# An attention block in two halves: a unit's products with V are issued three steps later, ahead of the next unit's turned maxima

## Chip, cores and metric

One core of one Trainium2 chip runs the whole kernel in one launch. The metric is the device time of an execution in microseconds (us). The kernel works in fp32, most products as three matmuls on upper and lower halves in fp32r.

## The reference, cut to what matters

```python
h = x + A(layernorm(x))            # S = 2048 tokens, D = 1024, H = 32 heads of 32, 4 segments of 512
# A, for each segment s and head:
logits = qs @ ks.T * scale + mask           # 512 x 512, causal
a_dot = softmax(logits) @ vs
a_mem = (phi(qs) @ M) / (phi(qs) @ z + 1e-6)   # M and z come from the segments before; 0 in segment 0
o = g * a_mem + (1 - g) * a_dot
M, z = M + phi(ks).T @ vs, z + phi(ks).sum()
# then o @ wo, and a block of layernorm, w1, gelu, w2 (channel MLP) over all tokens
```

## The kernel before

The sequence is done in two halves of 1,024 tokens. In each half the attention comes first, then the product with `wo`, then the MLP. The attention of a half has 16 **units** (n = 0 to 15), each one group of four heads (`g`) and one segment of 512 tokens (`sl` is 0 or 1). Units alternate so that segment 0 of a group comes before its segment 1. Segment `s = 2*half + sl`; only units with `s > 0` read the memory M. In the first half these are the eight units n = 2, 3, 5, 7, 9, 11, 14, 15; in the second half all sixteen.

The kernel's code is one long hand-written order. Every engine executes its instructions in program order. A unit has 24 **steps** (`b = 24 * n` is its first). In each step TensorE (PE) runs the three matmuls (`mm3`) of one of the 24 pieces of this unit's K, Q and V projections, and then `close(step)` runs what has been put down for that step with `at(step, ...)`, in the order in which it was put down: what unit n put down stands ahead of what unit n+1 put down. Last in `close` comes at most one small matmul from the list `small` (`one_small`). So the attention of a unit runs beside the projections of the units after it:

- `qk1` (steps 22 to 44 of the unit): logits of one block of rows into a PSUM bank "qk"; VectorE (DVE) adds the mask and takes the row maximum (L571); one step later ScalarE (ACT) takes exp for the row sums (L573).
- `lse` and `halves` (47, 48): logarithm of the sums, and the maxima in two halves `mh` (L601).
- `turn` (50): four matmuls turn `mh` into the tile `ptn` (L607), in one of two banks "pt". `rows` (51 to 54) copies it four times into rows 96 to 103 of `qs`, one copy a step, in turn by ACT, DVE, ACT, DVE (L610). Each copy waits for the one before it.
- `qk2` (53 to 67): logits again, transposed, with the maxima in the contraction (L619), into a bank "pst" of the same tag "pt"; ACT takes exp into `e` (L622); GpSimd (POOL) clears what the mask hides (L626). The first piece is in step 53, the second in step 54.
- `av` (71): sixteen products of `e` with V, 32 stationary columns each, one bank `po` (L633; four passes, so 32 matmul records of half a product each). `out` two steps on (73): DVE scales `po` by the gate and adds the memory's part (L642; L644 in segment 0). `out_high` (74): ACT copies the upper half (L651). `out_low` (75): POOL takes the lower half (L654). `store` (77): two DMAs by the queue of SP (L658), for n < 13.
- `reads` (26): puts four small matmuls `pm` on the list; after the second and the fourth, three DVE operations finish a half of the memory's part (L469 to L473).
- `stack` (steps 9 to 24): DMAs that lay K and Q of a head under each other (L417). `wload` (2, 7, 15 of every second unit): DMAs of weights (L688).

Step 71 of unit n is the step in which unit n+2 does its last piece of V's projection (step 23 of n+2). Step 74 is step 2 of unit n+3 and step 50 of unit n+1; unit n+2 is then at its step 26.

Of the kernel before, what the change touches and what calls it, by code (L numbers as in the profile page):

```python
# [39 lines left out]
LSE, TURN, ROWS, AV, LAST = 47, 50, (51, 52, 53, 54), 71, 432 + 8  # L40
# [11 lines left out]
def build(tc, x, wq, wk, wv, wo, beta, w1, b1, w2, b2, out):  # L52
# [307 lines left out]
    def attention(half, first):  # L360
# [15 lines left out]
        def at(step, *fns):  # L376
            assert step >= now[0], (step, now[0])
            todo.setdefault(step, []).extend(fns)
# [281 lines left out]
        def heads(u, b):  # L660
            for m, (j, i) in QK1.items():
                at(b + m, partial(qk1, u, j, i))
            at(b + QK0, partial(qk0, u))
            at(b + LSE, partial(lse, u))
            at(b + LSE + 1, partial(halves, u))
            at(b + TURN, partial(turn, u))
            for j, m in enumerate(ROWS):
                at(b + m, partial(rows, u, j))
            for m, (j, n) in QK2.items():
                at(b + m, partial(qk2, u, j, n))  # L670
            at(b + AV, partial(av, u))
            at(b + AV + 2, partial(out, u))
            at(b + AV + 3, partial(out_high, u))
            at(b + AV + 4, partial(out_low, u))
            if u["n"] < 13:
                at(b + AV + 6, partial(store, u))

        def close(step):

# [39 lines left out]
        for n in range(16):  # L719
            u = unit(n)  # L720
            heads(u, 24 * n)
            g, sl = ORDER[n]
            b = 24 * n
# [850 lines left out]
```

## Time and profile before

| | us |
|---|---|
| median of 3 runs (lowest, highest) | 2185.76 (2185.12, 2187.62) |
| the profiled execution | 2187.23 |
| its span, first to last instruction | 2185.5 |
| PE busy in the span | 2157.7 |

In the timelines a row is one instruction or several alike: its start in us from the span's start, how long it took, engine, line, operation, what it writes and reads, and in brackets how long the engine had been idle before and what ended that. A matmul of 512 columns has a row of 0.39 to 0.40 us, but the next one may start 0.23 us after it: rows of PE overlap, and only the distance between starts tells what a matmul takes. PEld is the loading of a matmul's stationary columns.

### The profile page before, as it was taken

The numbers are of one execution on the slowest core, as the hardware profiler recorded it, in microseconds if no ns is written. First come the engines' busy times: TensorE is split into PE (matmuls) and PEld (weight loads), VectorE is DVE, ScalarE is ACT, GpSimd is POOL, SyncE is SP. The second block draws the span as 40 slices with busy tenths as digits, with TensorE's granted clock in tenths as the row PEclk, the third lists the DMA queues.
The fourth block names the chain that finished last, engine by engine and source line by source line (L and its number), as shares of the span: only waits on it lengthen the run. The fifth ranks groups of instructions, "written<-read, shape, count | busy, mean of one in ns | idle before, by whom it ended". The sixth has DMA issues, their size and how long they took to land.

```text
span 2185.5 us, 33210 instructions
## 1 busy us (share of the span) xinstructions
PE 2157.7 (99%) x10937; PEld 1750.4 (80%) x10937; DVE 1349.0 (62%) x2696; ACT 1102.1 (50%) x2433; POOL 959.7 (44%) x1206
## 2 busy tenths in 40 slices
PE   7999999999999999999999999999999999999999
PEld 6777777778888888877777768888887888888887
DVE  6766666665745556766667655745666665576653
ACT  5777777762543445777777752643443232322221
POOL 5534345562444434533335561534446544256330
PEclk9999999999999999999999999999999999999999
DMA  6544445664465655544444663575569865676762
GB/s 182 134 106 107 105 107 136 190 203 164 154 207 155 187 158 147 136 107 109 106 108 133 198 197 141 173 217 162 171 199 373 274 226 185 190 244 230 250 222 92
DMA packets 352405, 376.20 MB, mean 172 GB/s; under 512 B 27214, under 2 KB 244330, under 8 KB 352234
## 3 DMA queue, kind: packets, MB, share of 16 engines
q1 hardware_dynamic: 288778, 336.98, 50.7%
q10 hardware_dynamic: 63456, 37.10, 5.6%
q8 instruction: 87, 1.43, 0.3%
q14 instruction: 84, 0.69, 0.1%
HBM read 241.27 MB, written 82.38 MB: 148 GB/s over the span
## 4 chain that ended last, share of the span: by engine, by line
PE 91%; DVE 2%; DMA 2%; POOL 2%; ACT 1%; issue 1%; SPq 0%; ACTq 0%; DVEq 0%; POOLq 0%
PE po L1410 22%; PE bps L1014 10%; PE cps L1014 7%; PE dps L1014 7%; PE pst L619 4%; PE po L633 3%; PE pqk L569 3%; PE kps L127 3%; PE vps L127 3%; PE qps L127 3%; PE kps L128 3%; PE pwo L127 2%; PE kps L129 2%; PE vps L128 2%; PE pwo L129 2%; PE pwo L128 2%
## 5 line engine op out<-in xcount | busy, mean ns | idle before, releaser
L571 DVE CUSTOM_DVE_ANT_0 pqk<-pqk,mask 128x512 f32<-128x512 f32 (+2 forms) x384 | 216.9, 565 | 241.6 <-PE pqk L569 214.8
L573 ACT ACTIVATE junk<-pqk,mx 128x512 f32<-128x512 f32 (+2 forms) x384 | 225.2, 587 | 134.7 <-DVE mx L571 128.2
L626 POOL TENSOR_SCALAR_AFFINE_SELECT e<-e 128x128 f32<-128x128 f32 (+1 forms) x384 | 137.6, 359 | 268.9 <-ACT e L622 254.1
L699 POOL TENSOR_TENSOR wl<-wr,wh 128x256 fp32r<-128x256 f32 x268 | 202.1, 770 | 108.7 <-PE pqk L569 85.8
L622 ACT ACTIVATE e<-pst 128x384 f32<-128x384 f32 (+1 forms) x384 | 200.8, 529 | 70.9 <-PE pst L619 69.5
L1420 DVE TENSOR_TENSOR c<-c,po 128x512 f32<-128x512 f32 x160 | 105.4, 684 | 156.7 <-PE po L1410 153.9
L569 PE MATMUL pqk<-ks,qs 96*128 96x512 f32 (+2 forms) x384 | 138.6, 361 | 5.7 <-ACT junk L573 3.0
L619 PE MATMUL pst<-qs,ks 104*128 104x512 f32 (+3 forms) x512 | 140.9, 318 | 1.0 <-ACT e L622 0.4
L619 PEld LDWEIGHTS pst<-qs,ks 104*128 104x128 f32 x512 | 95.7, 188 | 34.7 <-ACT e L622 10.7
L1410 PE MATMUL po<-w2h,zh 128*128 128x512 f32 x378 | 120.9, 389 | 0.4 <-DVE zh L1350 0.4
L1267 POOL TENSOR_TENSOR w2r<-w2r 128x512 f32<-128x512 f32 x54 | 84.6, 1579 | 72.3 <-DMA w2r<-in_B_w 72.3
L127 PE MATMUL kps<-yh,wh 128*128 128x512 f32 (+1 forms) x264 | 113.5, 430 | 0.0
L127 PE MATMUL qps<-yh,wh 128*128 128x512 f32 x256 | 113.2, 442 | 0.0
L1014 PE MATMUL bps<-zh,sb 128*128 128x512 f32 x336 | 110.9, 391 | 0.0
L1014 PE MATMUL bps<-zh,sa 128*128 128x512 f32 x336 | 110.8, 390 | 0.0
L1126 POOL TENSOR_TENSOR s<-r 128x512 f32<-128x512 f32 x28 | 44.3, 1583 | 141.0 <-DVE sa L1142 81.3
L127 PE MATMUL vps<-yh,wh 128*128 128x512 f32 x256 | 105.0, 410 | 0.0
L1410 PE MATMUL po<-w2h,hl 128*128 128x512 f32 x322 | 103.2, 390 | 0.7 <-DVE hl L1350 0.4
L128 PE MATMUL kps<-yl,wh 128*128 128x512 f32 (+1 forms) x264 | 102.8, 389 | 0.5 <-DVE yl L165 0.4
L129 PE MATMUL kps<-yh,wl 128*128 128x512 f32 (+1 forms) x264 | 102.2, 387 | 0.0
L128 PE MATMUL qps<-yl,wh 128*128 128x512 f32 x256 | 101.0, 394 | 0.0
L128 PE MATMUL vps<-yl,wh 128*128 128x512 f32 x256 | 100.8, 394 | 0.0
(271 smaller groups left out, 6204.0 us busy)
## 6 DMA issues: line engine op xcount, KB each, us to landing
hr<-h_dram SPq DMA_DIRECT2D x112, 448.0 KB, 5.5
w2r<-in_B_w SPq DMA_DIRECT2D x122, 256.0 KB, 4.2
r<-in_B_w SPq DMA_DIRECT2D x56, 512.0 KB, 4.6
ks<-kk SPq DMA_DIRECT2D x360, 64.0 KB, 2.0
qs<-qq SPq DMA_DIRECT2D x360, 64.0 KB, 2.0
h_dram<-ht ACTq DMA_DIRECT2D x84, 256.0 KB, 3.6
wx<-in_B_w SPq DMA_DIRECT2D x56, 256.0 KB, 3.5
o_dram<-side SPq DMA_DIRECT2D x52, 256.0 KB, 4.2
```

The costliest lines, as they stand in the source:

```text
L127: nc.tensor.matmul(ps, ah, bh, start=first, stop=False)
L128: nc.tensor.matmul(ps, ah, bl, start=False, stop=False)
L129: acts["mm"] = nc.tensor.matmul(ps, al, bh, start=False, stop=last)
L569: nc.tensor.matmul(ps, u["qs"][0:96, j, i * P:(i + 1) * P], u["ks"][0:96, j, 0:n], start=True, stop=True)
L571: nc.vector.tensor_tensor_reduce(out=ps, in0=ps, in1=mask[:, 512 - n:512], op0=ALU.add, op1=ALU.min, scale=-SCALE, scalar=3.0e38, accum_out=m)
L573: at(now[0] + 1, lambda: nc.scalar.activation(acts["junk"][:, :n], ps, AF.Exp, bias=m, scale=-1.0, accum_out=u["mx"][:, 1, i, j:j + 1]))
L619: nc.tensor.matmul(ps[:, o:o + 512 - P * jk], u["ks"][:, j, jk * P:(jk + 1) * P], u["qs"][:, j, jk * P:512], start=True, stop=True)
L622: nc.scalar.activation(e, ps[:, :w], AF.Exp, scale=SCALE)
L626: nc.gpsimd.affine_select(d, d, pattern=[[0, 2], [1, P]] if n == 2 else [[1, P]], compare_op=ALU.is_ge, fill=0.0, base=0, channel_multipli ...
L699: nc.gpsimd.tensor_tensor(l[:, c], wr[:, c], raw(h)[:, c], op=ALU.subtract)
L1014: nc.tensor.matmul(ps, x_[:, c, :], y_[:, c, :], start=first and c == 0 and n == 0, stop=last and c == 3 and n == 2, skip_group_check=True)
L1410: nc.tensor.matmul(ps, x_[:, k], y_[k], start=opens and k == 0 and i == 0, stop=closes and k == self.KP - 1 and i == 2, skip_group_check=True)
```

## The change

For units n < 15 the products with V are put down for step 24 + TURN = 74 in place of AV = 71, and `out`, `out_high`, `out_low` and `store` stay two, three, four and six steps behind them (76, 77, 78 and 80). In step 74 of unit n stands the `turn` of unit n+1; since unit n put its `av` down earlier, `av` comes directly ahead of it. Unit 15 keeps step 71. Thirty units of the 32 move.

```diff
-            at(b + AV, partial(av, u))
-            at(b + AV + 2, partial(out, u))
-            at(b + AV + 3, partial(out_high, u))
-            at(b + AV + 4, partial(out_low, u))
+            m = b + (24 + TURN if u["n"] < 15 else AV)
+            at(m, partial(av, u))
+            at(m + 2, partial(out, u))
+            at(m + 3, partial(out_high, u))
+            at(m + 4, partial(out_low, u))
             if u["n"] < 13:
-                at(b + AV + 6, partial(store, u))
+                at(m + 6, partial(store, u))
```

## Rows read from the trace of the kernel before

**Rows 1.** The page's first part: busy time, share and instructions of each engine.

```profile
PE 2157.7 (99%) x10937; PEld 1750.4 (80%) x10937; DVE 1349.0 (62%) x2696; ACT 1102.1 (50%) x2433; POOL 959.7 (44%) x1206
```

**Rows 2.** One source line each, whole span: count, duration in ns (least/median/most).

```profile
L633 PE MATMUL po<-e,vf x1024: 272/432/617, 90.9 to 1307.6; 128*32 128x512 f32 x43, 128*32 128x256 f32 x43, 128*32 128x128 f32 x43, 128*32 128x384 f32 x42
...
L607 PEld LDWEIGHTS ptn<-identr,mh x128: 85/88/88, 68.5 to 1290.4; 128*8 128x8 f32 x128
...
L473 DVE TENSOR_TENSOR om<-pm,rg x48: 424/424/426, 97.8 to 1269.0; 128x256 f32<-128x256 f32 x48
```

**Rows 3.** Timeline of PE: products with V of unit 3, then turned maxima of unit 4.

```profile
173.14 0.40 PE L129 MATMUL vps<-yh,wl 128*128 128x512 f32 x1
173.47 2.36 PE L633 MATMUL po<-e,vf 128*32 128x512 f32 x32
175.76 0.50 PE L127 MATMUL kps<-yh,wh 128*128 128x512 f32 x1
176.10 0.39 PE L128 MATMUL kps<-yl,wh 128*128 128x512 f32 x1
176.33 0.39 PE L129 MATMUL kps<-yh,wl 128*128 128x512 f32 x1
...
177.90 0.39 PE L129 MATMUL kps<-yh,wl 128*128 128x512 f32 x1
178.13 0.41 PE L607 MATMUL ptn<-identr,mh 128*8 128x128 f32 x4
```

**Rows 4.** Timeline of PEld in the same stretch.

```profile
175.76 0.19 PEld L127 LDWEIGHTS kps<-yh,wh 128*128 128x128 f32 x1 [0.20 <-DVE mh L601]
...
177.90 0.43 PEld L607 LDWEIGHTS ptn<-identr,mh 128*8 128x8 f32 x4
```

**Rows 5.** Timeline of DVE around a turn without reads, and around one with.

```profile
207.41 0.68 DVE L610 CAST qs<-ptn 8x512 fp32r<-8x512 f32 x1 [0.23 <-ACT qs L610]
...
1073.43 0.74 DVE L642 SCALAR_TENSOR_TENSOR side<-po,few,omt 128x512 f32<-128x512 f32 x1
...
1076.34 0.42 DVE L473 TENSOR_TENSOR om<-pm,rg 128x256 f32<-128x256 f32 x1
1076.80 0.68 DVE L610 CAST qs<-ptn 8x512 fp32r<-8x512 f32 x1
```

**Rows 6.** Timeline of ACT in the same two stretches.

```profile
209.29 0.60 ACT L622 ACTIVATE e<-pst 128x512 f32<-128x512 f32 x1 [0.59 <-PE pst L619]
...
1074.24 0.61 ACT L651 CAST side<-side 128x512 fp32r<-128x512 f32 x1
1074.87 0.57 ACT L610 CAST qs<-ptn 8x512 fp32r<-8x512 f32 x1
...
1077.52 0.57 ACT L610 CAST qs<-ptn 8x512 fp32r<-8x512 f32 x1 [1.48 <-DVE qs L610]
1078.11 0.60 ACT L622 ACTIVATE e<-pst 128x512 f32<-128x512 f32 x1
```

**Rows 7.** Timeline of PE: the second piece of qk2 behind three such turns.

```profile
100.23 0.44 PE L619 MATMUL pst<-qs,ks 104*128 104x384 f32 x1
...
1078.47 0.40 PE L129 MATMUL kps<-yh,wl 128*128 128x512 f32 x1
1078.77 0.45 PE L619 MATMUL pst<-qs,ks 104*128 104x384 f32 x1
...
1269.19 0.44 PE L619 MATMUL pst<-qs,ks 104*128 104x384 f32 x1 [0.20 <-ACT e L622]
```

**Rows 8.** Timeline of POOL, stretch with reads.

```profile
1074.93 1.29 POOL L654 TENSOR_TENSOR side<-side 128x512 fp32r<-128x512 f32 x1 [7.36 <-ACT side L651]
```

**Rows 9.** Timeline of SP's DMA issues, same stretch.

```profile
1076.17 1.03 SPq L658 DMA_DIRECT2D o_dram<-side  x2
1077.25 0.47 SPq L688 DMA_DIRECT2D wr<-in_A_wq  x1
1081.73 2.33 SPq L417 DMA_DIRECT2D ks<-kk  x3
```

## The prediction

> **What bounds the kernel now.** I read the page first: PE is busy for 99% of the span [rows 1], so what counts is what PE has to issue, and where its stream is held up. A held-up PE hardly shows as idle here, because a matmul's row of 0.39 us outlasts the 0.23 us in which the next may start. So I went on to the timeline of PE and read distances between starts, at the two places that the change joins: the products with V, and the turned maxima with what follows them. Then I read DVE and ACT behind the turned maxima, since PE waits for their work there.
>
> The products with V are 1024 records [rows 2], 32 for each of 32 units. Around them [rows 3] the reader is to see three distances. An ordinary matmul of 512 columns is followed 0.23 us on (176.10 to 176.33). From the last one ahead of the products to their start it is 0.33 (173.14 to 173.47): going in costs 0.10. The products take 2.29 (173.47 to 175.76). The matmul behind them is followed 0.34 us on, not 0.23 (175.76 to 176.10): going out costs 0.11. The loads say why the last is so [rows 4]: the 128 columns behind the products begin to load at 175.76, together with their matmul, while the maxima's load begins at 177.90, 0.23 ahead of their matmul at 178.13. So behind the products a load isn't hidden, and elsewhere it is. The way in and the products take the same to 0.01 us at all 32 places. PE waits for no data there.
>
> At the maxima, take the unit with its turn at 1074.14. The chain from there to the second piece of qk2 goes through two engines. DVE ends the first half of the memory's part (1076.34, 0.42 long) and at once copies row 1 at 1076.80 [rows 5]; ACT, idle for 1.48 until that copy is done, copies row 2 at 1077.52 and at once takes exp of the first piece at 1078.11 [rows 6]; PE starts the second piece at 1078.77, 0.30 behind the matmul ahead of it instead of 0.23 [rows 7]. This piece reuses the bank of the first, so it waits for that exp. The chain has no slack: PE is held up by 0.07 already. It is so in all 22 moved units in whose `out` step the unit two on reads the memory (48 such operations [rows 2] are 24 units, two a unit; units 0 and 1 of the second half have none moved before them); the first and the last of these 22 second pieces are at 100.23 and 1269.19 [rows 7]; only the last of each half is held up for longer, as the 0.20 of idle time at 1269.19 shows.
>
> **The change part by part.** *The products.* 30 of the 32 units move. Their 2.29 us and the 0.10 for going in remain, since a 512-column matmul stands ahead of them in either place. Going out changes: behind them now come the maxima, with 8 stationary columns a load, not 128. Loads last 88 ns [rows 2] against 0.19 us [rows 4], so about 0.10 of the 0.11 that is exposed goes. The bounds are 0 (any load costs the same exposed time) and 0.11 (nothing is exposed); I take 0.10 by the two durations, 30 x 0.10 = 3.0 us gained.
>
> *What the step leaves behind.* In steps 72 and 73 PE runs 2.4 us sooner after step 71, and the turn comes at the same time as before, with the products as its cover. What PE meets sooner, projections and one `qk1`, finds its weights and its bank free: that bank's exp was put down for step 69.
>
> *`out`.* It moves from step 73 to 76 on DVE and there stands ahead of the copy of row 1, which the next unit put down. At 73 nothing on PE's path stood behind it. At 76 it stands in the chain just read. It can't slide forward into DVE's idle time, because the memory's operations of step 75 stand ahead of it in order, and they wait for PE. So it starts where row 1 did, at 1076.80. From the rows of its old place [rows 5, 6]: `out_high` starts 0.81 after `out` (1073.43 to 1074.24), the next ACT copy 0.63 after that (1074.24 to 1074.87). So row 2 starts at 1076.80 + 0.81 + 0.63 = 1078.24. By way of row 1 it is the same: 0.74 for `out` and 0.72 from row 1 to row 2 give 1078.26. Then exp at + 0.59 and the second piece at + 0.66: 1079.49, against 1078.77. The hold-up grows by 0.72. Bounds: 0 if `out` were free after all; 0.74 + 0.63 = 1.37 if `out` and `out_high` stood in the chain one after the other. I take 0.72, since both ways through the rows agree. 22 x 0.72 = 15.8 us lost.
>
> *Units without reads.* There (6 units) ACT is idle for 0.59 ahead of exp of the first piece, at 209.29, waiting for PE itself [rows 6]. DVE is idle for 0.23 before row 1 at 207.41 [rows 5], so `out` starts at 207.18 at the latest, row 2 at 207.18 + 0.81 + 0.63 = 208.62 and exp could start at 209.21, before 209.29. Nothing is lost, with 0.08 to spare; at worst some 0.1 x 6 = 0.6 us. Unit 14 of each half has no reads behind it either, and more idle time: nothing.
>
> *`out_high`, `out_low`, `store`.* ACT's 0.61 is in the chain above. POOL's 1.29 [rows 8] moves behind the first masked piece of the next unit, whose readers come some 20 steps later, and nothing on PE waits for it. SP's two issues go from 1076.17 to behind the weights at 1077.25, and must be out before K's stack at 1081.73 [rows 9], some 1081.73 + 0.7 after the change. `out_low` would end by about 1080.9 in this unit (1077.61 for `out_high`, 0.61, an exp and mask of about 1 us, 1.29), the two issues by 1082. At worst the stack is 0.5 us late, and its first reader is 13 steps, some 14 us, later: nothing.
>
> *Sum.* On the span 2185.5 + 15.8 - 3.0 = 2198.3; the profiled execution had 1.7 around its span, so it would read 2200.0. The median of the runs was 1.5 below that execution: 2198.5.
>
> *A rule weighed.* The rows show that the maxima are entered at the ordinary 0.23 with their load ahead of them [rows 3, 4]; so they save nothing by standing next to the products but the hidden load, and the sum stays at 2198.5. The Trainium skill, in TensorEngine Tiling (Array Packing), section Tiling Modes, says that a change of tiling mode drains TensorE and a change of the tile alone does not. By that rule, if the maxima with their 8 columns ran in the mode of the products, one way in and one way out would go, and the sum would be 2195.2. The trace agrees with the rule at the products, where going in costs 0.10, and shows no such change at the maxima.
>
> **The rivals.** *Nothing is held up* (0.08): only the loads' 3.0 is left, 2182.7. It needs DVE or the bank to be free in a way that the rows don't show; against it, the chain of copies has ACT waiting for DVE, by name, in the row at 1077.52.
>
> *The other side, two ways in and out become one* (0.04): products and maxima belong together for PE, so that 0.10 going in and 0.11 going out go per unit, 30 x 0.21 = 6.3, and the hold-up is hidden: 2179.5. It is decided at the maxima and the matmul behind them: no 0.11 on either. The rule of the Trainium skill weighed above would make it so. For it: the cost at the products is real. Against it: the maxima's load runs ahead of them now [rows 4], so there is no way in to be saved. Should this saving come with the hold-up, the time is 2198.5 + 3.0 - 6.3 = 2195.2, within the range.
>
> *The hold-up grows* (0.08): ACT gets 0.61 more in the stretch in which its rows are back to back, and the next pieces wait too, up to the 1.37 of above: 22 x 1.37 - 3.0 = 27.1, 2212.9. Against it: ACT was idle for 1.48 just before, and PE is late by then as well.
>
> **How the numbers follow.** The likeliest (0.80) is the sum: 2198.5, by itself 2195 to 2202 (0.15 a unit either way). The range leaves out the first two rivals (0.12) and most of the third, and takes in the side case of 2195.2 and half of the third's growth: 2193 to 2206. Changes under 0.2% (4.4 us) are about what a measurement of this kernel can't tell from none. The sum is slower by 0.58%. Slower 0.88 (sum and growth), within 0.2% 0.08 (nothing held up: -0.14%), faster 0.04 (two ways become one: -0.29%).
>
> **What would show it.** Right: in 22 units the second piece of qk2 starts some 1.0 behind the matmul ahead of it instead of 0.30, and the group of its 104x384 matmuls gets some 13 us of idle time, ended by ACT's exp; DVE has `out` between the memory's first half and row 1; the matmul behind the products (now the maxima) has no 0.11 extra, and the projections of step 72 start at 0.23. The 6 units without reads keep their distances. Wrong: `out` ahead of the memory's operations, a second piece that comes at 0.30 as before, or hold-ups of PE at other places (the third piece, K's stack).

## The result, and the profile after

The changed kernel takes 2196.66 us (median of 5, 2193.73 to 2196.94), the kernel before 2185.2 in the same session: ratio 1.0045, 95% interval 1.0034 to 1.0056. The forecast was 2198.5, in a range of 2193 to 2206. The profiled execution took 2196.94, its span 2195.2, so the span grew by 9.7.

PE's busy time did not grow; it fell from 2157.7 [rows 1] to 2154.5. The page's first part and, from the groups of PE matmuls between 60 and 1320 us, the matmuls of `qk2` of the form 104x384, four a unit, of which the first is the second piece:

```profile
PE 2154.5 (98%) x10937; PEld 1748.7 (80%) x10937; DVE 1360.4 (62%) x2696; ACT 1104.8 (50%) x2433; POOL 954.2 (43%) x1206
```

```profile
L619 PE MATMUL pst<-qs,ks 104*128 104x384 f32 x128 | 46.4, 363 | 13.1 <-ACT e L622 12.8
```

Behind the second bar stands the idle time ahead of the group: 13.1 us, 12.8 of it ended by ACT's exp. The view of waits counts them:

```profile
PE pst L619 <- ACT e L622: 12.8, 22, 0.9
```

22 times, the number of places with reads. One of them, the same unit as in [rows 5 to 7], now with its turn at 1080.02. DVE, ACT and PE, each its timeline:

```profile
1082.21 0.42 DVE L473 TENSOR_TENSOR om<-pm,rg 128x256 f32<-128x256 f32 x1
1082.55 0.74 DVE L642 SCALAR_TENSOR_TENSOR side<-po,few,omt 128x512 f32<-128x512 f32 x1
1083.32 0.68 DVE L610 CAST qs<-ptn 8x512 fp32r<-8x512 f32 x1
```

```profile
1083.33 0.62 ACT L651 CAST side<-side 128x512 fp32r<-128x512 f32 x1 [1.54 <-DVE side L642]
1084.04 0.57 ACT L610 CAST qs<-ptn 8x512 fp32r<-8x512 f32 x1
1084.64 0.60 ACT L622 ACTIVATE e<-pst 128x512 f32<-128x512 f32 x1
```

```profile
1084.35 0.40 PE L129 MATMUL kps<-yh,wl 128*128 128x512 f32 x1
1085.29 0.44 PE L619 MATMUL pst<-qs,ks 104*128 104x384 f32 x1 [0.55 <-ACT e L622]
```

`out` stands between the memory's operations and the copy of row 1; row 2 starts at 1084.04, 0.04 after row 1 is done (1083.32 + 0.68) and 0.09 after `out_high` is (1083.33 + 0.62). The second piece comes 0.94 behind the matmul ahead of it, where it came 0.30 behind it [rows 7]. Counted from the turn, it is at 5.27, before at 1078.77 - 1074.14 = 4.63: 0.64 more.

Where the products are left, PE and PEld of the unit of [rows 3, 4]:

```profile
174.20 0.40 PE L127 MATMUL kps<-yh,wh 128*128 128x512 f32 x1
174.44 0.40 PE L128 MATMUL kps<-yl,wh 128*128 128x512 f32 x1
...
176.24 0.39 PE L129 MATMUL kps<-yh,wl 128*128 128x512 f32 x1
176.56 2.36 PE L633 MATMUL po<-e,vf 128*32 128x512 f32 x32
178.85 0.40 PE L607 MATMUL ptn<-identr,mh 128*8 128x128 f32 x4
179.09 0.33 PE L569 MATMUL pqk<-ks,qs 96*128 96x256 f32 x1
```

```profile
178.85 0.22 PEld L607 LDWEIGHTS ptn<-identr,mh 128*8 128x8 f32 x4 [0.20 <-issue]
```

The first projection of step 72 (174.20) is followed 0.24 on, not 0.34. Going in still costs 0.09 (176.24 to 176.56 is 0.32). The maxima's load now begins together with their matmul, at 178.85, as that of 128 columns did; but the four matmuls still take 0.24 (178.85 to 179.09), so this load costs nothing that can be seen.

### The profile page after: what moved, and what is told of

It is laid out like the page before. It is cut to its first block, busy times and chain, and to the rows that moved or that the text cites. A ratio compares the mean times of both kernels' runs of the same rounds, so it can differ in the third digit from the quotient of the medians.

```text
span 2195.2 us, 33207 instructions
## 1 busy us (share of the span) xinstructions
PE 2154.5 (98%) x10937; PEld 1748.7 (80%) x10937; DVE 1360.4 (62%) x2696; ACT 1104.8 (50%) x2433; POOL 954.2 (43%) x1206
## 4 chain that ended last, share of the span: by engine, by line
PE 86%; DVE 4%; ACT 3%; DMA 2%; issue 2%; POOL 1%; SPq 1%; ACTq 0%; DVEq 0%; POOLq 0%
PE po L1411 21%; PE bps L1015 10%; PE cps L1015 7%; PE dps L1015 6%; PE pst L619 3%; PE po L633 3%; PE pqk L569 3%; PE qps L127 3%; PE pwo L127 2%; PE pwo L128 2%; PE pwo L129 2%; PE vps L127 2%; PE qps L128 2%; PE qps L129 2%; PE vps L128 2%; PE vps L129 2%
## 5 line engine op out<-in xcount | busy, mean ns | idle before, releaser
L619 PE MATMUL pst<-qs,ks 104*128 104x512 f32 (+3 forms) x512 | 140.9, 318 | 13.1 <-ACT e L622 12.8
L619 PEld LDWEIGHTS pst<-qs,ks 104*128 104x128 f32 x512 | 95.7, 188 | 48.6 <-ACT e L622 27.6
```

Of the source, the lines that this page charges most:

```text
L619: nc.tensor.matmul(ps[:, o:o + 512 - P * jk], u["ks"][:, j, jk * P:(jk + 1) * P], u["qs"][:, j, jk * P:512], start=True, stop=True)
```

## Experiments

The ratios are to the kernel before, run on the same chip in the same session; they are taken over all the runs, and the quotient of two medians differs from them by up to 0.0007. Beside them stands what a unit costs in the stretch where it is cleanest: 13 units of the second half, all with reads, from the turn of its unit 1 to that of its unit 14 (starts of L607 in PE's timeline). In the kernel before it is 1264.57 - 911.40 = 353.17.

| | ratio (95% interval) | turn 1 to turn 14 | more than before, per unit |
|---|---|---|---|
| changed kernel | 1.0045 (1.0034 to 1.0056) | 359.66 | +0.50 |
| e1: `out` behind rows 1 and 3 | 0.9972 (0.9962 to 0.9983) | 351.30 | -0.14 |
| e2: `out` alone moved | 1.0058 (1.0045 to 1.0070) | 361.63 | +0.65 |
| e3: products behind the turn | 0.9999 (0.9991 to 1.0008) | 353.08 | -0.01 |
| e4: `out` twice | 1.0108 (1.0095 to 1.0122) | 370.44 | +1.33 |
| e5: only `out` in step 76 | 1.0034 (1.0022 to 1.0047) | 359.78 | +0.51 |
| e6: `out` directly behind row 1 | 0.9977 (0.9968 to 0.9986) | 351.42 | -0.13 |
| e7: as e6, `out_high` ahead of row 2 | 1.0147 (1.0133 to 1.0160) | 369.72 | +1.27 |
| e8: `store` alone moved | 0.9998 (0.9989 to 1.0006) | 353.75 | +0.04 |

The theory: the products' new place is a gain, and the loss is `out` on DVE ahead of the copy of row 1. The rivals: the products' place holds PE up; ACT's `out_high` does it; products and maxima belong together for PE; the DMAs' place matters.

**e1, the changed kernel with `out` and what follows it three steps later still.**

```diff
+            k = 3 if u["n"] < 15 else 0
             at(m, partial(av, u))
-            at(m + 2, partial(out, u))
-            at(m + 3, partial(out_high, u))
-            at(m + 4, partial(out_low, u))
+            at(m + 2 + k, partial(out, u))
+            at(m + 3 + k, partial(out_high, u))
+            at(m + 4 + k, partial(out_low, u))
             if u["n"] < 13:
-                at(m + 6, partial(store, u))
+                at(m + 6 + k, partial(store, u))
```

> The changed kernel with only `out`, `out_high`, `out_low` and `store` three steps later still (79, 80, 81, 83), so that DVE copies rows 1 and 3 of the turned maxima ahead of `out`; the products with V stay at 74, ahead of the turn. Theory (the 0.64 us by which the second piece of qk2 comes later in 22 units is `out` ahead of the copy of row 1 on DVE): the hold-up goes, about 14 us less than the changed kernel, and the hidden load remains as a gain of 0.1 a unit, so about 3 us under the kernel before: 2182. Rival (the products directly ahead of the turn hold up PE, whatever DVE does): stays near 2196. Second rival (`out` only moves the wait on, to the third piece of qk2 or the bank of the products): between, 2188 to 2194.

Measured 2180.03 against 2186.52. The hold-up is gone, as DVE's and PE's timelines of the same unit show (turn at 1068.70):

```profile
1070.89 0.42 DVE L473 TENSOR_TENSOR om<-pm,rg 128x256 f32<-128x256 f32 x1
1071.34 0.68 DVE L610 CAST qs<-ptn 8x512 fp32r<-8x512 f32 x1
...
1075.00 0.75 DVE L642 SCALAR_TENSOR_TENSOR side<-po,few,omt 128x512 f32<-128x512 f32 x1
```

```profile
1073.03 0.40 PE L129 MATMUL kps<-yh,wl 128*128 128x512 f32 x1
1073.31 0.45 PE L619 MATMUL pst<-qs,ks 104*128 104x384 f32 x1
```

The second piece is 0.28 behind the matmul ahead of it, and of PE's 22 waits for exp the view of waits has two left:

```profile
PE pst L619 <- ACT e L622: 0.5, 2, 0.2
```

By its interval this version is faster than both kernels, if only by 0.28% against the kernel before. The rival of the products' place falls.

**e2, the kernel before with only `out`, `out_high`, `out_low` and `store` three steps later.** The diff is that of e1 with `b + AV` in place of `m`.

> The kernel before with only `out`, `out_high`, `out_low` and `store` three steps later (76, 77, 78, 80); the products with V stay at 71. Theory (`out` on DVE): the whole loss and none of the gain, 22 x 0.64 = 14 us over the kernel before, 2199, or up to 1 to 2 us less where a later wait takes some of it in. Rival (the place of the products on PE): as the kernel before, 2185.

Measured 2198.89, 12.4 over the kernel before of its session: the whole loss without the change's main line, 0.65 a unit. (22 x 0.65 would be 14.3; the interval, 9.8 to 15.3 us, holds both.) The view of waits reads as that of the changed kernel:

```profile
PE pst L619 <- ACT e L622: 12.8, 22, 0.9
```

**e3, as e1, but the products directly behind the turn in step 74.**

```diff
             at(b + TURN, partial(turn, u))
+            if u["n"]:
+                at(b + TURN, partial(av, U[u["n"] - 1]))
```

The diff is cut here: the old line of `av` stays for unit 15 alone, and the lines of e1 are in it too.

> As the first of this call (`out` late), but the products with V stand directly behind the turn in step 74 instead of directly ahead of it. Theory (the gain is the load of 8 columns in place of one of 128 right behind the products): the gain goes, about 0.1 a unit or 3 us over the first of this call, 2185, since one load of 128 columns is exposed again. Rival (products and turn belong together for PE, and standing side by side saves a way in and a way out): the same time as the first of this call, 2182, and no 0.10 for going in.

Measured 2186.21, 6.2 us over e1 where 3 were expected: no gain is left in the time. PE's timeline:

```profile
172.21 0.39 PE L129 MATMUL kps<-yh,wl 128*128 128x512 f32 x1
172.44 0.40 PE L607 MATMUL ptn<-identr,mh 128*8 128x128 f32 x4
172.77 2.36 PE L633 MATMUL po<-e,vf 128*32 128x512 f32 x32
175.06 0.39 PE L569 MATMUL pqk<-ks,qs 96*128 96x256 f32 x1
175.29 0.39 PE L408 MATMUL pm<-MZ,pq 128*128 128x132 f32 x2
```

The maxima go in at 0.23 as ever. From them to the products it is 0.33, where the four take 0.24: the 0.09 for going in is there, with the maxima as neighbour too. And `qk1` behind the products, 256 columns of 96 rows with 128 columns to load, is followed 0.23 us on. PE's timeline of the kernel before has such a `qk1` in two other places:

```profile
170.96 0.28 PE L569 MATMUL pqk<-ks,qs 96*128 96x256 f32 x1
171.08 0.39 PE L127 MATMUL vps<-yh,wh 128*128 128x512 f32 x1
...
178.37 0.34 PE L569 MATMUL pqk<-ks,qs 96*128 96x256 f32 x1
178.54 0.39 PE L408 MATMUL pm<-MZ,pq 128*128 128x132 f32 x2
```

Away from products and maxima it is followed 0.12 on, behind the maxima 0.17. So the load of 128 columns costs 0.11 behind the products here as well, of which some 0.05 had been paid behind the maxima before. Products and maxima do not belong together for PE; what counts is what must be loaded behind the products.

The gain of a unit is not gone whole. The -0.01 of the table holds two units in which PE waits (0.57 longer than before, with a wait for ACT's `lse`, and 0.22 longer, with one of the turn); in the eleven between them a unit costs 0.08 less than before, where e1 saves 0.14. 30 times that difference of 0.06 are 1.8 of the 6.2. Another 3.6 is a wait that this order opens, in the view of waits:

```profile
PE ptn L607 <- DVE mh L601: 3.6, 3, 1.7
```

Behind the turn, the products no longer cover the maxima's own way through ACT and DVE, and in three units, the last of each half above all, the turn waits for them.

**e4, the changed kernel with `out` done twice** (in moved units of segments 1 to 3).

```diff
-                nc.vector.scalar_tensor_tensor(ot, po, gate_, u["omt"], op0=ALU.mult, op1=ALU.add)
+                for _ in range(2 if u["n"] < 15 else 1):
+                    nc.vector.scalar_tensor_tensor(ot, po, gate_, u["omt"], op0=ALU.mult, op1=ALU.add)
```

> The changed kernel with `out` done twice in the moved units of segments 1 to 3 (the same result written twice); 18 of them stand in the 22 places with reads, two in places without. Theory: `out` is in the chain to the second piece of qk2, so the hold-up there grows by another 0.67 in 18 units, and by some 0.5 in two: about 13 us over the changed kernel, 2209 to 2210. Rival (DVE has time there, the hold-up is ACT's `out_high` or PE's own): 2197 to 2200.

Measured 2210.18. DVE and PE:

```profile
1092.00 1.53 DVE L643 SCALAR_TENSOR_TENSOR side<-po,few,omt 128x512 f32<-128x512 f32 x2
1093.56 0.69 DVE L610 CAST qs<-ptn 8x512 fp32r<-8x512 f32 x1
```

```profile
1095.52 0.44 PE L619 MATMUL pst<-qs,ks 104*128 104x384 f32 x1 [1.33 <-ACT e L622]
```

The idle time of PE went from 0.55 to 1.33, by 0.78; `out` from 0.74 to 1.53, by 0.79. What DVE does there comes out on PE one to one. (One of the 13 units of the table is 0.5 longer than its like; the others cost 1.29 more than before, 0.50 + 0.79.)

**e5, the changed kernel with `out` in step 76 and `out_high`, `out_low`, `store` three steps later.** The diff is that of e1 without the line of `out`.

> The changed kernel with `out` left in step 76, ahead of the copy of row 1, and only `out_high`, `out_low` and `store` three steps later (80, 81, 83). Theory (the wait goes through DVE: row 2 on ACT starts 0.035 us after row 1 is done, and `out_high` is done 0.1 before that): nothing changes, 2195 to 2197. Rival (ACT's upper half ahead of row 2 sets the hold-up): the hold-up goes, 2181 to 2183.

Measured 2193.67, some 1.3 below what was expected, a small miss, with an interval that overlaps that of the changed kernel. A unit costs the same (0.51 against 0.50), and so does the wait of PE. ACT and PE:

```profile
1082.40 0.57 ACT L610 CAST qs<-ptn 8x512 fp32r<-8x512 f32 x1 [2.25 <-DVE qs L610]
1082.99 0.60 ACT L622 ACTIVATE e<-pst 128x512 f32<-128x512 f32 x1
```

```profile
1083.64 0.44 PE L619 MATMUL pst<-qs,ks 104*128 104x384 f32 x1 [0.54 <-ACT e L622]
```

ACT is idle for 2.25 ahead of row 2 and waits for DVE alone: `out_high` is not the cause.

**e6, `out` directly behind row 1 in step 76, the rest as in e1.**

```diff
                 at(b + m, partial(rows, u, j))
+                if j == 1 and u["n"]:
+                    at(b + m, partial(out, U[u["n"] - 1]))
```

The diff is cut here: the old line of `out` stays for unit 15 alone.

> As the changed kernel, but in step 76 DVE copies row 1 first and does `out` directly behind it; `out_high`, `out_low` and `store` three steps later (80, 81, 83), out of ACT's way. Theory (what counts is that `out` stood ahead of row 1): no hold-up beyond that of the kernel before, the gain of the hidden load remains, as with `out` at 79, 2180 to 2183. Rival (DVE is short of time in these steps, so any 0.7 us more there comes back through the maximum of step 76 or row 3): 2185 to 2192.

Measured 2181.58, as e1 within what the intervals tell apart. DVE and PE:

```profile
1073.54 0.68 DVE L610 CAST qs<-ptn 8x512 fp32r<-8x512 f32 x1
1074.26 0.75 DVE L642 SCALAR_TENSOR_TENSOR side<-po,few,omt 128x512 f32<-128x512 f32 x1
```

```profile
1075.22 0.40 PE L129 MATMUL kps<-yh,wl 128*128 128x512 f32 x1
1075.51 0.44 PE L619 MATMUL pst<-qs,ks 104*128 104x384 f32 x1
```

The second piece is 0.29 behind the matmul ahead of it. One place in the order of one step makes the difference to e5; DVE has the time for `out` there.

**e7, as e6, with `out_high` in step 77, where it stands ahead of row 2 on ACT.** The diff is that of e6 with `out_high`, `out_low` and `store` left at `m + 3`, `m + 4` and `m + 6`.

> As the one before it in this call (`out` directly behind row 1 on DVE in step 76), but with `out_high` in step 77 as in the changed kernel, where it stands ahead of row 2 on ACT; `out_low` 78 and `store` 80. Theory (the chain in order decides, and now `out` and `out_high` stand in it one after the other): row 2 about 1.3 us later than without them, so 22 x 1.3 = 28.6 in the places with reads and some 6 x 0.5 = 3 in those without, less the gain of 4: 2211 to 2215. Rival (ACT passes over an instruction that is not ready): as the one before it, 2180 to 2183.

Measured 2217.88, above the 2211 to 2215 expected. DVE, ACT and PE:

```profile
1095.90 0.68 DVE L610 CAST qs<-ptn 8x512 fp32r<-8x512 f32 x1
1096.62 0.75 DVE L642 SCALAR_TENSOR_TENSOR side<-po,few,omt 128x512 f32<-128x512 f32 x1
```

```profile
1097.40 0.62 ACT L651 CAST side<-side 128x512 fp32r<-128x512 f32 x1 [2.38 <-DVE side L642]
1098.05 0.57 ACT L610 CAST qs<-ptn 8x512 fp32r<-8x512 f32 x1
1098.65 0.60 ACT L622 ACTIVATE e<-pst 128x512 f32<-128x512 f32 x1
```

```profile
1099.30 0.44 PE L619 MATMUL pst<-qs,ks 104*128 104x384 f32 x1 [1.31 <-ACT e L622]
```

Row 1 is done at 1096.58, and ACT stands idle ahead of `out_high`, which waits for `out`; only behind it may it copy row 2, at 1098.05. `out` and `out_high` are in the chain one after the other, and a unit costs 1.27 + 0.13 = 1.40 more than in e6, where 1.3 was expected (`out` starts only when row 1 is done). Here the view of waits has 30 such waits and 35.7 us: the eight places without reads pay too. By the starts of L607 and L619 the second piece comes 0.64 later after its turn than before in six of them and 1.12 later in the two at the ends of the halves, where 0.5 in six had been expected; with the 1.40, that is where the miss comes from.

**e8, the kernel before with `store` alone at step 80.**

```diff
-                at(b + AV + 6, partial(store, u))
+                at(b + AV + 9, partial(store, u))
```

> The kernel before with `store` alone three steps later (80), behind the weights of step 79 in SP's queue. It tells what the place of the DMAs is worth, since some waits of PE for qs became shorter in the changed kernel. Theory: nothing that can be told apart, 2184 to 2187. Rival (the order in SP's queue takes away PE's waits for qs): 1 to 3 us under the kernel before.

Measured 2185.9 against 2186.77, ratio 0.9998: the place of the DMAs in SP's queue is worth nothing that can be told. The +0.04 of the table is one unit alone, 0.55 longer, in which PE waits for a stacked Q; the other twelve are as before within 0.05. Its profiled span was 2183.0 all the same, 2.5 less than that of the kernel before. The spans of the kernel before itself, 22 runs beside e5 to e8, lie between 2181.2 and 2188.1, so no such difference of two single spans is read as a cause here.

## Why the prediction was right

**What bounds the kernel, and the chain.** Right: no slack in the chain DVE row 1, ACT row 2, exp, second piece. e4 shows it most directly, e2 and e6 show that it is `out`'s place in it and nothing else of the change.

**The hold-up's size.** Forecast 0.72 in 22 places, 15.8 in all; measured 0.64, 14.1. The step that was over-sized is the start of `out`: I put it where row 1 had started, 0.03 to 0.04 after the memory's operation was done, 2.66 after the turn. It starts 0.08 before that is done (1082.55 against 1082.21 + 0.42), 2.53 after the turn. Row 1 then comes 0.77 behind `out`, not 0.74, and from there on the rows hold. `out_high` is then out of the way in time, so only one of the two ways through the rows, that by row 1, sets row 2; e5 confirms it.

**The gain.** Forecast 0.10 a unit, 3.0 in all; by e1, where nothing covers it, 0.14 a unit, 4.2 in all. That is above the upper bound of 0.11, which had the load alone in it. Three distances account for most: the projection behind the old place 0.10 to 0.11 shorter, going in 0.01 shorter (0.32 against 0.33), and the way from the turn to the second piece 0.02 shorter (1073.31 - 1068.70 = 4.61 against 4.63). e3 shows that it hangs on what is loaded behind the products.

**The sum.** With the measured sizes 14.1 - 4.2 = 9.9 on the span, which grew by 9.7; forecast 12.8. Both errors were on the same side, so the forecast came out too high. That 9.9 and 9.7 lie so close is luck in part, by what e8 says of single spans: by the medians the time grew by 11.5, by the ratio of the runs by 9.8, with an interval of 7.4 to 12.2.

**Units without reads.** Right: the 22 waits leave none for the six. In the one of [rows 5, 6], exp of the first piece starts 0.18 after ACT is free, waiting for PE:

```profile
209.73 0.57 ACT L610 CAST qs<-ptn 8x512 fp32r<-8x512 f32 x1
210.49 0.60 ACT L622 ACTIVATE e<-pst 128x512 f32<-128x512 f32 x1 [0.18 <-PE pst L619]
```

**POOL and SP.** Right: `out_low` ends 6.84 after the turn (forecast 1080.9 - 1074.14 = 6.8), and K's stack is issued 8.24 after it instead of 7.59, later by the hold-up alone. In POOL's and SP's timelines:

```profile
1085.57 1.29 POOL L654 TENSOR_TENSOR side<-side 128x512 fp32r<-128x512 f32 x1
```

```profile
1088.26 4.18 SPq L417 DMA_DIRECT2D ks<-kk  x4
```

**The rivals.** Nothing held up: it is what e1 and e6 are, not the change. Two ways in and out become one: in the change itself the 0.11 that is gone behind the products would fit this rival too; e3 decides against it, since going from the maxima to the products costs the 0.09. The hold-up grows: not in the change; e7 shows the order in which it does.

**Left open.** By medians e1 is 6.5 us faster than the kernel before, and 30 units of 0.14 are 4.2. The interval of its ratio is 3.7 to 8.3 us, so the runs don't show that there is more than the 4.2. If there is, waits of PE for the stacked Q may hold some of it (2.4 us in the kernel before, 1.3 in e1, 1.4 in e8, by the views of waits of the attention); one execution of each was profiled, and no run here settles what sets them.

## What to carry to other kernels

When a step is moved, look at what it brings to every engine's queue in its new place, not only at the engine for which it is moved: the products' gain of 0.14 was real, and 0.7 us of a follow-up on another engine, put ahead of one short copy, cost over four times that in each of 22 places. Where a kernel's order is written by hand, find the chain without slack first (here: the copies that feed the next matmuls) and put everything else behind it in the same step. A busy share of 99% doesn't show such a chain; distances between starts do.

## What the runs showed of the hardware that was not expected

- Behind the products with 32 stationary columns a load isn't hidden, and what it costs differs with its columns: 0.11 us for 128 (0.34 against 0.23 start to start [rows 3], and 0.23 against 0.12 at `qk1` in e3), nothing visible for 8 (178.85 to 179.09, as before the change). No other width was seen there. Going in costs 0.09 to 0.10 whether 128-column projections or 8-column maxima stand ahead.
- On DVE `out` began 0.08 us before the operation ahead of it was done, in every one of the 22 places with reads, while in the kernel before the copy of row 1 behind the same operation began 0.03 to 0.04 after; such a difference is worth 22 x 0.1 us here.
